# Attention in steps of two items: scores and outputs of a pair share PSUM banks, and the order of a step is rewritten

## The chip, the cores and the metric

One core of a Trainium2 chip. The metric is the device time of one execution in microseconds (us). Engines: PE is TensorE (matmuls; transposes are matmuls with an identity), DVE is VectorE, ACT is ScalarE, POOL is GpSimd, SP issues DMAs. Every engine works through its own queue in order and waits there for semaphores of the others.

## What is computed

Attention in a window of 128 positions over q, k, v of shape (4, 8, 576, 64), then a mixture of 8 experts whose gate is balanced over all tokens, then a dense block:

```
scores = where(0 <= i - j < 128, q k^T / 8 - slope_h |i - j|, -1e9)
x      = softmax(scores) v                        # 2304 tokens x 512
P      = exp(x w_gate - max); 8 times: P /= rows, P /= columns, P *= N / E
x      = sum_e P[:, e] * (relu(x w1[e]) w2[e])
out    = g(x w_in) w_out                          # g: 0, (h + 1)^2 / 4, h
```

## The kernel before

To keep float32 accuracy every large matmul is three: an operand is kept as a high part (fp32r) and a low part, and high x high, low x high and high x low add up in one PSUM bank (`mm3`, lines 72 to 75).

**Attention** goes by items (g, i): g is one of 16 pairs of heads (4 batches x 4 pairs), i one of 5 blocks of query rows (4 of 128 rows, the last of 64); 80 items. One item passes through five stages, each a function:
- `a_scores` (S): for each of two heads three matmuls over 64 rows of the array, into one bank per head (`s0`, `s1`); then on DVE per head one instruction that adds the bias and takes the row maximum (line 290), and a small negation (293).
- `a_exp` (E): two exps on ACT (300). `a_norm` (N): 1/sum on DVE (306, 307), multiplication on POOL (308).
- `a_turn` (T): transposes of the weights on PE (320), copied out by ACT (first key block, 324) and DVE (second, 326).
- `a_out` (O): weights times v on PE, each head into 64 columns of the array (338); high part of the result on ACT (341), low part on DVE (342).

Beside them run `a_prep` (P: transposes of q and k on PE, line 264, one bank `p`; high parts on ACT, 270; low parts on DVE, 271), in three parts per pair of heads; B, which advances the splitting of weights for the first expert (ACT line 78, POOL line 79); and F, the **fill-in**: groups of three matmuls of the first expert's first half (`u0_g1`, `u0_g2`) and of the gate (`logits`: lines 351 and 358), which need only tokens whose attention is done. `blocks` says after which item each block of tokens may start, `credit` and `SHARE` how many groups a step gets. What fill-in is left runs after attention; then come the other experts and the dense block, bound by PE.

The order is written by hand: step s works on item s in S, on s - OE in E, s - ON in N, s - DT in T and s - DO in O, in the order of the letters of `START` (first 19 steps) or `ORDER`; `PREP0` and `PREP` say at which step each preparation stands.

Of the kernel before, what the change touches and what calls it, by code (L numbers as in the profile page):

```python
# [19 lines left out]
P = 128  # L20
# [8 lines left out]
def attn_moe_ffn(ctx: ExitStack, tc, q, k, v, w_gate, w1, w2, w_in, w_out, out):  # L29
# [243 lines left out]
    def a_scores(g, i, ap, bias):  # L273
        h0 = 2 * (g % NPAIR)
        q0, nq = QB[i]
        k0 = max(0, q0 - P)
        nk = q0 + nq - k0
        c0 = P if i == 0 else 0
        s = ap.tile([P, 2, 2 * P], F32, tag="s", bufs=DT + 1, name="s")
        mx = ap.tile([P, 8], F32, tag="mx", bufs=DT + 2, name="mx")  # L280
        (qh, ql), (kh, kl) = QK[g, "q"], QK[g, "k"]
        pss = []
        for j in range(2):
            hs = slice(j * D, (j + 1) * D)
            ps = ps_pools[0].tile([P, 2 * P], F32, tag=f"s{j}", bufs=1, name="pss")
            pss.append(ps)
            mm3(ps[:nq, :nk], qh[hs, q0:q0 + nq], ql[hs, q0:q0 + nq], kh[hs, k0:k0 + nk], kl[hs, k0:k0 + nk],
                True, True)
        for j in range(2):
            nc.vector.tensor_tensor_reduce(  # L290
                out=s[:nq, j, :nk], in0=pss[j][:nq, :nk], in1=bias[:nq, h0 + j, c0:c0 + nk], scale=1.0,
                scalar=-3.0e38, op0=ALU.add, op1=ALU.max, accum_out=mx[:nq, j:j + 1])
        nc.vector.tensor_scalar(mx[:nq, 2:4], mx[:nq, 0:2], -1.0, None, ALU.mult)
        st[g, i] = (s, mx, nk)
# [16 lines left out]
    def a_turn(g, i, ap):  # L311
# [4 lines left out]
        at = ap.tile([P, 2, 2, P], F32, tag="at", bufs=DO - DT + 1, name="at")  # L316
# [12 lines left out]
    def a_out(g, i):  # L329
        b, hp = divmod(g, NPAIR)  # L330
        q0, nq = QB[i]
        at, kbs = atT.pop((g, i))
        o = ps_pools[0].tile([P, P], F32, tag="o", bufs=1, name="pso")
        for j in range(2):
            hs = slice(j * D, (j + 1) * D)
            for c, kb in enumerate(kbs):
                n = QB[kb][1]
                nc.tensor.matmul(o[hs, :nq], lhsT=nat[b, "v", kb][:n, (2 * hp + j) * D:(2 * hp + j + 1) * D], rhs=at[:n, c, j, :nq],  # L338
                                 start=(c == 0), stop=(c == len(kbs) - 1))
        cs = slice(b * SQ + q0, b * SQ + q0 + nq)  # L340
        nc.scalar.activation(xh[:, hp, cs], o[:, :nq], AF.Copy)
        nc.vector.tensor_tensor(xl[:, hp, cs], o[:, :nq], xh[:, hp, cs].bitcast(F32), ALU.subtract)
# [396 lines left out]
    DT, DO, OE, ON = 3, 4, 1, 1  # L739
    START, ORDER, NSTART = "EBSNFPOT", "BFESNPFOT", 19  # L740
    SHARE = 1.8
    PREP0 = [-1, 3, 4, 0, 5, 6, 1, 7, 8, 2, 9, 10]
    PREP = [11, 14, 17, 20, 29, 34, 37, 41, 53, 56, 59, 67]
    LAG = (5, 4, 4, 4, 4, 4, 6, 4)
    with tc.manual_schedule():
# [11 lines left out]
        preps = [(y, *divmod(n, 3)) for n, y in enumerate(PREP0)]  # L757
        preps += [(PREP[g - NPAIR] + x, g, x) for g in range(NPAIR, NG) for x in range(3)]
# [9 lines left out]
        with tc.tile_pool(name="ac", bufs=1, side="right") as ac, tc.tile_pool(name="ap", bufs=2, side="right") as ap, \  # L768
# [8 lines left out]
            ri = ap.tile([P, 2 * P], mybir.dt.int32, tag="s", bufs=DT + 1, name="ri")  # L777
# [34 lines left out]
            gated = []  # L812
# [12 lines left out]
            work, credit, step = unit0(), 0.0, [0]  # L825
            for s in range(NI + DO):
                step[0] = s
                order = START if s < NSTART else ORDER
                for op_ in order:
                    off = {"S": 0, "E": OE, "N": ON, "T": DT, "O": DO}.get(op_, 0)  # L830
                    if not 0 <= s - off < NI and op_ in "SENTO":
                        continue
                    g, i = items[min(s - off, NI - 1)]
                    if op_ == "S":
                        a_scores(g, i, ap, bias)
                        if s < 2:
                            for h in range(2, 6) if s == 0 else range(6, H):
                                make_bias(h)
                        if s == 3:
                            for x in range(NPAIR, NPAIR + 2):  # L840
                                a_load(x, ap)
                        if s == 2:
                            fast.append(u0_weights(wp))
                        if s == 9:
                            fast.append(gate_setup())
                    elif op_ == "E":
                        a_exp(g, i)
                    elif op_ == "N":
                        a_norm(g, i)
                    elif op_ == "T":  # L850
                        a_turn(g, i, ap)
# [9 lines left out]
                    elif op_ == "P":  # L861
                        if s == max(PREP0) + 1:
# [3 lines left out]
                        for _, pg, x in (y for y in preps if y[0] == s):  # L866
# [3 lines left out]
                    elif op_ == "O":  # L870
                        a_out(g, i)
                        if (g + 1) % NPAIR == 0 and g + 1 < NG:
                            for x in [i - 1] if i < NQ - 1 else [i - 1, i]:
                                if x >= 0:
                                    v_load((g + 1) // NPAIR, x, ap)
            while state == "open":
                state = next(work)
            step[0] = 2 * NI
# [96 lines left out]
```

## Time and profile before

| | us |
|---|---|
| median of 3 runs | 2126.49 (2126.47 to 2130.02) |
| the profiled execution, its own time | 2127.65 |
| its span in the profile | 2125.9 |
| PE, DVE, ACT, POOL busy | 2085.9, 1318.9, 672.1, 615.5 |

The page gives means over the whole span. The attention part is its first 255 us; there the busy time of an engine is to be read by stretches, and a matmul by the distance from its start to the next one's: matmuls are pipelined, so the length of one (0.28 us for 256 columns) is longer than what it costs in a run.

### The profile page before, as it was taken

Reading aid. Unit: us, or ns where it says so; the run is one execution under the profiler, and the core shown is the slowest. Engines: PE = TensorE matmul, PEld = TensorE weight load, DVE = VectorE, ACT = ScalarE, POOL = GpSimd, SP = SyncE. Lnnn points to the kernel's source line nnn. Section 1 sums busy time; section 2 is a strip of 40 time slices with the busy share of each in tenths; the row PEclk is TensorE's granted clock in tenths of the full one; section 3 lists DMA queues with packets and bytes.
Section 4 is the critical chain, followed back from the end, with each engine's and each line's share of the span. In section 5 each row is a group of like instructions: output and inputs, shape, how many; then the busy total and the mean of one; then the engine's idle time right before and its main releaser. Section 6 shows DMA issues by size and latency. Waiting matters only on the chain.

```text
span 2125.9 us, 30586 instructions
## 1 busy us (share of the span) xinstructions
PE 2085.9 (98%) x11187; PEld 1838.8 (86%) x11187; DVE 1318.9 (62%) x2999; ACT 672.1 (32%) x1601; POOL 615.5 (29%) x619
## 2 busy tenths in 40 slices
PE   8999999999999999999999999999999999999999
PEld 5777779998998898998998899899899988888887
DVE  6766484544454666666665765766665567767665
ACT  6666534333333332121121132121121133232322
POOL 4332226666666631011111110111110022232322
PEclk9999999999999999999999999999999999999999
DMA  7322136767677676766676566676665445464542
GB/s 140 76 70 60 42 124 255 280 249 257 240 266 265 209 265 245 256 244 223 240 249 223 214 226 241 242 257 232 225 242 208 175 177 183 169 221 154 204 183 104
DMA packets 179622, 432.46 MB, mean 203 GB/s; under 512 B 69648, under 2 KB 93200, under 8 KB 179472
## 3 DMA queue, kind: packets, MB, share of 16 engines
q1 hardware_dynamic: 168112, 411.37, 55.2%
q10 hardware_dynamic: 11360, 19.14, 2.8%
q8 instruction: 88, 1.44, 0.3%
q14 instruction: 62, 0.51, 0.1%
HBM read 311.44 MB, written 119.01 MB: 202 GB/s over the span
## 4 chain that ended last, share of the span: by engine, by line
PE 88%; DVE 7%; ACT 2%; DMA 1%; issue 1%; POOL 0%; DVEq 0%; ACTq 0%; POOLq 0%
PE psg L73 16%; PE psg L75 15%; PE psg L74 15%; PE psc L73 3%; PE psd L73 3%; PE psc L74 3%; PE psd L74 3%; PE psc L75 3%; PE psd L75 3%; PE pso L338 3%; PE psa L74 3%; PE psa L75 3%; PE psa L73 3%; PE psb L73 2%; PE psb L74 2%; PE psb L75 2%
## 5 line engine op out<-in xcount | busy, mean ns | idle before, releaser
L75 PE MATMUL psg<-w2h,hl 128*128 128x512 f32 x1368 | 534.5, 391 | 0.8 <-POOL hl L628 0.5
L73 PE MATMUL psg<-w2h,hh 128*128 128x512 f32 x1368 | 533.7, 390 | 0.9 <-DVE acc L686 0.9
L74 PE MATMUL psg<-w2l,hh 128*128 128x512 f32 x1368 | 532.3, 389 | 0.0
L686 DVE SCALAR_TENSOR_TENSOR acc<-psg,pt,acc 128x512 f32<-128x512 f32 x252 | 188.1, 749 | 254.4 <-PE psg L75 252.8
L75 PEld LDWEIGHTS psg<-w2h,hl 128*128 128x128 f32 x1368 | 256.8, 188 | 58.6 <-POOL hl L628 5.4
L73 PEld LDWEIGHTS psg<-w2h,hh 128*128 128x128 f32 x1368 | 256.8, 188 | 51.5 <-DVE acc L686 1.3
L74 PEld LDWEIGHTS psg<-w2l,hh 128*128 128x128 f32 x1368 | 256.9, 188 | 51.0
L628 POOL TENSOR_TENSOR hl<-g,hh 128x384 fp32r<-128x384 f32 x96 | 111.6, 1171 | 280.7 <-ACT hh L626 262.0
L73 PE MATMUL psc<-xh,w1h 128*128 128x384 f32 x456 | 156.5, 343 | 17.9 <-DVE u L641 17.9
L615 ACT ACTIVATE hh<-c 128x384 fp32r<-128x384 f32 x270 | 140.8, 522 | 88.6 <-DVE c L652 57.7
L617 DVE SCALAR_TENSOR_TENSOR hl<-c,hh 128x384 fp32r<-128x384 f32 x270 | 160.1, 626 | 0.0
L75 PE MATMUL psc<-xh,w1l 128*128 128x384 f32 x456 | 154.8, 340 | 0.0
L74 PE MATMUL psc<-xl,w1h 128*128 128x384 f32 x456 | 154.7, 339 | 0.0
L73 PE MATMUL psd<-sh,w1h 128*128 128x384 f32 x456 | 153.5, 337 | 0.8 <-DVE c L644 0.8
L74 PE MATMUL psd<-sl,w1h 128*128 128x384 f32 x456 | 153.0, 336 | 0.0
L75 PE MATMUL psd<-sh,w1l 128*128 128x384 f32 x456 | 152.9, 335 | 0.0
L79 POOL TENSOR_TENSOR dl<-e,dh 128x128 fp32r<-128x128 f32 (+1 forms) x64 | 43.1, 682 | 356.7 <-ACT dh L78 356.7
L635 ACT ACTIVATE p<-psa 128x384 f32<-128x384 f32 x57 | 28.1, 493 | 343.1 <-PE psa L75 340.9
L308 POOL TENSOR_TENSOR s<-s,mx 128x512 f32<-128x512 f32 (+2 forms) x80 | 72.9, 911 | 153.1 <-DVE mx L307 70.0
L79 POOL TENSOR_TENSOR w2l<-raw,w2h 128x512 fp32r<-128x512 f32 x60 | 81.3, 1377 | 104.4 <-ACT w2h L78 104.4
L73 PEld LDWEIGHTS psc<-xh,w1h 128*128 128x128 f32 x456 | 85.6, 188 | 22.3 <-DVE u L641 22.2
L638 DVE TENSOR_TENSOR u<-psb,p 128x384 f32<-128x384 f32 x57 | 31.8, 557 | 116.5 <-PE psb L75 96.5
(198 smaller groups left out, 4183.1 us busy)
## 6 DMA issues: line engine op xcount, KB each, us to landing
w1h<-wd1h SPq DMA_DIRECT2D x84, 896.0 KB, 4.6
w1l<-wd1l SPq DMA_DIRECT2D x84, 896.0 KB, 6.8
w2h<-wd2h SPq DMA_DIRECT2D x84, 512.0 KB, 5.1
w2l<-wd2l SPq DMA_DIRECT2D x84, 512.0 KB, 6.2
raw<-in_moe_w SPq DMA_DIRECT2D x60, 512.0 KB, 4.5
wd1h<-w1h SPq DMA_DIRECT2D x30, 896.0 KB, 6.2
wd1l<-w1l SPq DMA_DIRECT2D x30, 896.0 KB, 6.4
wd2h<-w2h SPq DMA_DIRECT2D x30, 512.0 KB, 6.2
```

What stands on the lines that cost most here:

```text
L73: nc.tensor.matmul(ps, lhsT=lh, rhs=rh, start=first, stop=False, skip_group_check=on)
L74: nc.tensor.matmul(ps, lhsT=lh, rhs=rl, start=False, stop=False, skip_group_check=on)
L75: nc.tensor.matmul(ps, lhsT=ll, rhs=rh, start=False, stop=last, skip_group_check=on)
L79: eng.tensor_tensor(l, x, h.bitcast(F32), ALU.subtract)
L308: nc.gpsimd.tensor_tensor(s[:nq, :, :nk], s[:nq, :, :nk], mx[:nq, 6:8].unsqueeze(2).to_broadcast([nq, 2, nk]), ALU.mult)
L338: nc.tensor.matmul(o[hs, :nq], lhsT=nat[b, "v", kb][:n, (2 * hp + j) * D:(2 * hp + j + 1) * D], rhs=at[:n, c, j, :nq], start=(c == 0), sto ...
L615: nc.scalar.activation(h, c, AF.Relu)
L617: V.scalar_tensor_tensor(l, c, 0.0, h.bitcast(F32), ALU.max, ALU.subtract)
L628: nc.gpsimd.tensor_tensor(l, g, h.bitcast(F32), ALU.subtract)
L635: nc.scalar.activation(p1, pa, AF.Copy)
L638: V.tensor_tensor(u2, pb, p1, ALU.add)
L686: nc.vector.scalar_tensor_tensor(a, ps, sc, a, ALU.mult, ALU.add)
```

## The change

A step now takes two items that follow one another. `a_scores` writes both items' scores of a head into one bank, head by head in turn, then reduces the two items; `a_out` writes both items' outputs into one bank, then takes high and low part of the first item and of the second. E, N and T run their two items one after the other. A step's order is S, T, P, N, E, B, P, O at first and S, T, P, N, E, F, B, F, P, O from step 6 on; exps belong to the same step as the scores (OE 0), turn and outputs to the one two steps back. At the first P one preparation part runs, at the last P all others that are due. Fill-in gets 3.6 groups a step and starts after the last preparation of the first batch is done (step 10).

```diff
+    def a_scores(two, ap, bias):
+        PS = [ps_pools[0].tile([P, 2, 2 * P], F32, tag=f"s{j}", bufs=1, name="pss") for j in range(2)]
...
+        for x, (g, i) in enumerate(two):
...
+            for n, (a, b) in enumerate(((qh, kh), (qh, kl), (ql, kh))):
+                for j in range(2):
+                    hs = slice(j * D, (j + 1) * D)
+                    nc.tensor.matmul(PS[j][:nq, x, :nk], lhsT=a[hs, q0:q0 + nq], rhs=b[hs, k0:k0 + nk],
+                                     start=n == 0, stop=n == 2)
+        for x, (g, i) in enumerate(two):
...
+            s = ap.tile([P, 2, 2 * P], F32, tag="s", bufs=6, name="s")
+            mx = ap.tile([P, 8], F32, tag="mx", bufs=8, name="mx")
...
-        at = ap.tile([P, 2, 2, P], F32, tag="at", bufs=DO - DT + 1, name="at")
+        at = ap.tile([P, 2, 2, P], F32, tag="at", bufs=4, name="at")
...
+    def a_out(two):
+        PS = ps_pools[0].tile([P, 2, P], F32, tag="o", bufs=1, name="pso")
+        for x, (g, i) in enumerate(two):
...
+                    nc.tensor.matmul(PS[hs, x, :nq], lhsT=nat[b, "v", kb][:n, (2 * hp + j) * D:(2 * hp + j + 1) * D],
+                                     rhs=at[:n, c, j, :nq], start=(c == 0), stop=(c == len(kbs) - 1))
+        for x, (g, i) in enumerate(two):
...
+            nc.scalar.activation(xh[:, hp, cs], o, AF.Copy)
+            nc.vector.tensor_tensor(xl[:, hp, cs], o, xh[:, hp, cs].bitcast(F32), ALU.subtract)
...
-    DT, DO, OE, ON = 3, 4, 1, 1
-    START, ORDER, NSTART = "EBSNFPOT", "BFESNPFOT", 19
-    SHARE = 1.8
-    PREP0 = [-1, 3, 4, 0, 5, 6, 1, 7, 8, 2, 9, 10]
+    DT, DO, OE, ON = 2, 2, 0, 1
+    START, ORDER, NSTART = "STPNEBPO", "STPNEFBFPO", 6
+    SHARE = 3.6
+    PREP0 = [-1, 2, 3, 0, 3, 4, 1, 5, 6, 2, 7, 8]
     PREP = [11, 14, 17, 20, 29, 34, 37, 41, 53, 56, 59, 67]
...
-        preps += [(PREP[g - NPAIR] + x, g, x) for g in range(NPAIR, NG) for x in range(3)]
+        preps += [((PREP[g - NPAIR] + x) // 2, g, x) for g in range(NPAIR, NG) for x in range(3)]
...
-                    while step[0] <= last + DO:
+                    while step[0] <= max(last // 2 + DO, max(PREP0) + 1):
...
-                        for _, pg, x in (y for y in preps if y[0] == s):
+                        now = [y for y in preps if y[0] <= s]
+                        for y in now[:1 if pos < order.rindex("P") else None]:
+                            preps.remove(y)
+                            _, pg, x = y
                             a_prep(pg, ap, x)
```

Smaller edits: the last six bias rows are all made in step 0, the loads of the second batch's first pairs and the weight splits are put in at step 1, the gate's setup at step 4.

Where the instructions stand, at three places. First PE in the middle of attention, between fill-in of 512 columns (psg; pss are scores, psat turned weights, pso outputs). Before, one item:

```order
L75 MATMUL psg<-w1h,hl 128x512
L73 MATMUL pss<-xl 128x256
...
L75 MATMUL pss<-xl 128x256
L73 MATMUL psg<-w1h,hh 128x512
...
L75 MATMUL psg<-w1h,hl 128x512
L338 MATMUL pso<-at,nv_138 64x64
...
L320 MATMUL psat<-ident,s 128x128 x2
L73 MATMUL psg<-w1h,hh 128x512
```

and now the end of one step and the start of the next:

```order
L75 MATMUL psg<-w1h,hl 128x512
L343 MATMUL pso<-at,nv_1064 64x128 [waits DVE_49,Activation_49]
L343 MATMUL pso<-at,nv_1161 64x128 [waits DMAHW2_49,DVE_49]
...
L343 MATMUL pso<-at,nv_1161 64x128 [waits Activation_49]
...
L286 MATMUL pss<-xh 128x256 x12
L324 MATMUL psat<-ident,s 128x64 [waits PE_49,Pool_49]
...
L324 MATMUL psat<-ident,s 128x128 [waits PE_49,Pool_49]
...
L264 MATMUL pst<-ident,nq 128x128 [waits DMAHW4_49]
...
L73 MATMUL psg<-w1h,hh 128x512
```

Scores of two items now follow outputs directly and lead straight into the turn; no fill-in stands between them.

Second, ACT's queue in one of the first steps. Before (item step; L300 are the exps, L270 the preparation, L341 the outputs' high part):

```order
L324 ACTIVATE at<-psat 128x256 [waits PE_49,Activation_49]
L300 ACTIVATE s,mx<-s,mx 128x256 [waits DVE_49,Pool_49]
...
L78 ACTIVATE w1h<-raw 128x512
L354 ACTIVATE L<-psl 16x256 [waits PE_49]
L270 ACTIVATE xh<-pst 128x512 [waits PE_49]
L341 ACTIVATE xh<-pso 128x128 [waits PE_49]
```

and now, step 5 (the same names, the exps on L304, the outputs on L350):

```order
L328 ACTIVATE at<-psat 128x256 [waits PE_49,Activation_49] x2
L270 ACTIVATE xh<-pst 128x256 [waits PE_49]
L270 ACTIVATE xh<-pst 128x256 [waits DVE_49]
L304 ACTIVATE s,mx<-s,mx 64x192 [waits Pool_49]
...
L304 ACTIVATE s,mx<-s,mx 128x256 [waits Pool_49]
...
L78 ACTIVATE w0h<-raw 128x512 [waits DMAHW0_49]
L270 ACTIVATE xh<-pst 128x512 [waits PE_49]
L350 ACTIVATE xh<-pso 128x128 [waits PE_49]
L350 ACTIVATE xh<-pso 128x128 [waits DVE_49]
```

The exps stood ahead of a step's preparation and now stand behind its first part, whose second copy waits for DVE; the second item's output copy waits for DVE too.

Third, DVE's queue of the same step (L294 reductions, L330 copy of turned weights, L271 preparation, L351 outputs' low part):

```order
L330 COPY at<-psat 128x256 [waits Activation_49]
L271 SCALAR_TENSOR_TENSOR xh<-pst,xh 128x256 [waits Activation_49] x2
L310 TENSOR_SCALAR mx<-mx 128x2
L311 RECIPROCAL mx<-mx 128x2 [waits DVE_49]
...
L271 SCALAR_TENSOR_TENSOR xh<-pst,xh 128x512 [waits Activation_49]
L351 TENSOR_TENSOR xl<-pso,xh 128x128 [waits Activation_49] x2
L294 ISA s,mx<-pss,bias 128x256 [waits PE_49,Pool_49]
```

The next step's first reduction (the last row) stands behind both low parts of this step's outputs.

## Rows read from the trace of the kernel before

**Rows 1.** The page, busy time of each engine with its share and instructions.

```profile
PE 2085.9 (98%) x11187; PEld 1838.8 (86%) x11187; DVE 1318.9 (62%) x2999; ACT 672.1 (32%) x1601; POOL 615.5 (29%) x619
```

**Rows 2.** Stretches: PE, PEld, DVE, ACT, POOL busy, PE clock, DMA.

```profile
7.30:41.40 34.10, 29.93 (x162) 20.91 (x162) 24.88 (x108) 20.98 (x77) 13.86 (x14) 1.00 0.84 166
...
68.90:243.60 174.70, 174.70 (x1429) 127.83 (x1428) 117.57 (x577) 114.85 (x419) 53.59 (x60) 1.00 0.24 60
...
276.90:280.40 3.50, 3.10 (x7) 2.48 (x8) 3.26 (x10) 1.94 (x4) 2.36 (x3) 0.51 0.38 147
```

**Rows 3.** Timeline of PE: first score matmuls of items 0, 20, 79; a spacing early.

```profile
7.30 0.47 PE L73 MATMUL pss<-xh 64*128 64x128 f32 x1 [1.35 <-ACT xh L270]
...
30.04 0.42 PE L74 MATMUL pss<-xl 64*128 64x256 f32 x2
30.26 0.42 PE L75 MATMUL pss<-xl 64*128 64x256 f32 x2
...
68.93 0.33 PE L73 MATMUL pss<-xh 64*128 64x128 f32 x2
...
243.61 0.31 PE L73 MATMUL pss<-kh,qh 64*64 64x192 f32 x2
```

**Rows 4.** Timeline of PE: start, length, instruction (xN: merged); lone groups, then a run.

```profile
152.55 0.39 PE L73 MATMUL pss<-xh 64*128 64x256 f32 x2
152.78 0.29 PE L74 MATMUL pss<-xh 64*128 64x256 f32 x2
152.89 0.28 PE L75 MATMUL pss<-xh 64*128 64x256 f32 x2
153.11 0.39 PE L73 MATMUL psg<-xh,w0h 128*128 128x256 f32 x1
...
153.67 0.67 PE L338 MATMUL pso<-at,nv 128*64 128x128 f32 x8
...
270.10 0.28 PE L73 MATMUL psg<-xh,w0h 128*128 128x256 f32 x1
...
270.44 0.28 PE L73 MATMUL psg<-xh,w0h 128*128 128x256 f32 x1
```

**Rows 5.** Timeline of DVE, then of ACT: one item's reductions and exps.

```profile
150.89 0.42 DVE L290 CUSTOM_DVE_ANT_0 s<-pss,bias 128x256 f32<-128x256 f32 x1 [0.76 <-PE pss L75]
...
151.78 0.16 DVE L306 TENSOR_SCALAR mx<-mx 128x2 f32<-128x2 f32 x1
...
150.22 0.50 ACT L300 ACTIVATE s<-s,mx 128x256 f32<-128x256 f32 x1
...
151.35 0.38 ACT L433 ACTIVATE hh<-psg 128x256 fp32r<-128x256 f32 x1
```

**Rows 6.** Groups by line and shape, 100 to 250 us: count, busy us, mean ns.

```profile
L342 DVE TENSOR_TENSOR xl<-pso,xh 128x128 fp32r<-128x128 f32 x41 | 11.7, 286 | 6.4 <-ACT xh L341 5.8
L341 ACT ACTIVATE xh<-pso 128x128 fp32r<-128x128 f32 x41 | 11.3, 277 | 14.5 <-PE pso L338 14.1
L271 DVE SCALAR_TENSOR_TENSOR ql<-pst,qh 128x512 fp32r<-128x512 f32 x6 | 4.1, 680 | 0.1
L270 ACT ACTIVATE qh<-pst 128x512 fp32r<-128x512 f32 x6 | 3.6, 594 | 1.0 <-PE pst L264 1.0
```

**Rows 7.** Timeline of ACT and DVE: a preparation of two matrices in one bank.

```profile
24.01 0.62 ACT L78 ACTIVATE w0h<-raw 128x512 fp32r<-128x512 f32 x1
24.95 0.38 ACT L270 ACTIVATE xl<-pst 128x256 fp32r<-128x256 f32 x1 [0.32 <-PE pst L264]
26.62 0.38 ACT L270 ACTIVATE xl<-pst 128x256 fp32r<-128x256 f32 x1 [1.29 <-DVE xl L271]
...
27.04 0.42 DVE L271 SCALAR_TENSOR_TENSOR xl<-pst,xl 128x256 fp32r<-128x256 f32 x1 [0.45 <-ACT xl L270]
```

**Rows 8.** Timeline of PE, 275 to 278 us: the waits before the clock fell.

```profile
275.30 0.50 PE L75 MATMUL psg<-w1h,hl 128*128 128x512 f32 x1 [1.58 <-DVE hl L434]
...
277.30 0.79 PE L75 MATMUL psg<-w1h,hl 128*128 128x512 f32 x1 [1.04 <-DVE hl L434]
```

More of the change, by code (lines that the diff above doesn't have):

```diff
@@ L271, in a_prep @@
             nc.vector.scalar_tensor_tensor(l, pc, scale, h.bitcast(F32), ALU.mult, ALU.subtract)
[L273 to L294, printed above, removed]
+    def a_scores(two, ap, bias):
+        PS = [ps_pools[0].tile([P, 2, 2 * P], F32, tag=f"s{j}", bufs=1, name="pss") for j in range(2)]
+        made = []
+        for x, (g, i) in enumerate(two):
+            q0, nq = QB[i]
+            k0 = max(0, q0 - P)
+            nk = q0 + nq - k0
+            made.append((nq, nk, P if i == 0 else 0))
+            (qh, ql), (kh, kl) = QK[g, "q"], QK[g, "k"]
+            for n, (a, b) in enumerate(((qh, kh), (qh, kl), (ql, kh))):
[4 more added lines that the diff above has]
+        for x, (g, i) in enumerate(two):
+            nq, nk, c0 = made[x]
+            h0 = 2 * (g % NPAIR)
+            s = ap.tile([P, 2, 2 * P], F32, tag="s", bufs=6, name="s")
+            mx = ap.tile([P, 8], F32, tag="mx", bufs=8, name="mx")
+            for j in range(2):
+                nc.vector.tensor_tensor_reduce(
+                    out=s[:nq, j, :nk], in0=PS[j][:nq, x, :nk], in1=bias[:nq, h0 + j, c0:c0 + nk], scale=1.0,
+                    scalar=-3.0e38, op0=ALU.add, op1=ALU.max, accum_out=mx[:nq, j:j + 1])
+            nc.vector.tensor_scalar(mx[:nq, 2:4], mx[:nq, 0:2], -1.0, None, ALU.mult)
+            st[g, i] = (s, mx, nk)
@@ L756, in attn_moe_ffn @@
         NI = len(items)
-        preps = [(y, *divmod(n, 3)) for n, y in enumerate(PREP0)]
-        preps += [(PREP[g - NPAIR] + x, g, x) for g in range(NPAIR, NG) for x in range(3)]
+        preps = [(y, *divmod(n, 3)) for n, y in enumerate(PREP0) if n]
+        preps += [((PREP[g - NPAIR] + x) // 2, g, x) for g in range(NPAIR, NG) for x in range(3)]
         blocks = [(7, 0, 256), (19, 256, 256), (27, 512, 256), (39, 768, 384), (47, 1152, 256), (59, 1408, 256),
@@ L775, in attn_moe_ffn @@
                 v_load(0, i, ap)
[L777 removed]
+            ri = ap.tile([P, 2 * P], mybir.dt.int32, tag="s", bufs=6, name="ri")
             nc.gpsimd.iota(ri, pattern=[[1, 2 * P]], base=-P, channel_multiplier=-1)
@@ L861, in attn_moe_ffn @@
                     elif op_ == "P":
-                        if s == max(PREP0) + 1:
+                        if s == max(PREP0) + 1 and not opened:
+                            opened.append(s)
                             p0.close()
@@ L870, in attn_moe_ffn @@
                     elif op_ == "O":
[L871 to L875, printed above, removed]
+                        a_out(two)
+                        for g, i in two:
+                            if (g + 1) % NPAIR == 0 and g + 1 < NG:
+                                for x in [i - 1] if i < NQ - 1 else [i - 1, i]:
+                                    if x >= 0:
+                                        v_load((g + 1) // NPAIR, x, ap)
             while state == "open":
                 state = next(work)
-            step[0] = 2 * NI
+            step[0] = NI
         spool = ctx.enter_context(tc.tile_pool(name="spool", bufs=1, side="right"))
```

56 lines of the change are left out of this document (28 added, 28 removed).

## The prediction, made before the changed kernel had run

> **What bounds the kernel now.** I read the page's busy times first. TensorE is busy 98% of the span and VectorE and ScalarE have much room [rows 1]; but these are means over stages, so I went to the stretches of the attention part next [rows 2], cut at the first score matmul of item 0, where that spacing halves, and at the first score matmuls of items 20 and 79 [rows 3]. The reader is to see three stages. From 7.3 to 41.4 us PE is busy 88% of the time although it has no fill-in yet, and at the lower of its two rates: score matmuls of 256 columns start 0.22 us apart at 30 us, 0.11 us apart at 152 us [rows 3, 4]. From 68.9 to 243.6 us, 59 items of attention with fill-in, PE shows no gap (174.7 of 174.7 us), while DVE and ACT are busy two thirds of it: this stage is bound by PE's issue, at 174.7 / 59 = 2.96 us an item. After it comes the dense mixture of experts, which the change does not touch.
>
> Then the single matmuls of one item, start to start [rows 4]. Three fill-in matmuls of 256 columns in a run take 0.34 us (270.10 to 270.44). The same three between scores and outputs take 0.56 us (153.11 to 153.67), and so does the score triple, whose two heads run side by side on 64 rows each (152.55 to 153.11). So what PE loses is at the borders between kinds of matmul: full array, two row halves (scores), two column halves (outputs). A lone group loses 0.22 us by its two borders, some 0.1 us on either side of each, and a border has two sides.
>
> **What the change saves on PE.** An item has four borders now: fill-in to scores, scores to fill-in, fill-in to outputs, outputs to turn (turn to fill-in is none: both use the full array). At 0.2 us for a border with scores or fill-in on both sides, and 0.15 for those of outputs and turn, whose first matmul is held up less, that is 0.7 us an item. After the change a step of two items has three: outputs to scores 0.2, scores to turn 0.15, fill-in to outputs 0.15, together 0.5, or 0.25 an item. It saves 0.45 an item, 0.9 a step: PE's own need falls from 2 x 2.96 = 5.92 us to 5.0 us a step. Matmuls, reductions, copies and bytes stay the same in number. The interleaving of the two heads' score matmuls costs and gains nothing, since the two heads already start 0.01 us apart (the x2 of these rows).
>
> **What it adds: two waits in series that PE's work now has to cover.** The exps come in the same step as the scores (OE 0 for 1), behind the step's first preparation in ACT's queue; the next step's reductions come behind the low parts of this step's outputs in DVE's queue; and two items share a bank. Durations, from X, the start of a step's first reduction on DVE:
> - Reductions and negation of one item hold DVE 0.89 us (150.89 to 151.78), of two 1.78; each reads a bank that is ready only after both items' scores. The exps of one item hold ACT about 1.0 us, 1.13 with the tail (150.22 to 151.35) [rows 5]; of two 2.1.
> - Outputs: high part on ACT 0.28, low part on DVE 0.28 [rows 6], and now high of the second item only after low of the first: 4 x 0.28 and hand-overs, 1.2 us.
> That last wait has a forerunner in the trace: of a preparation with two matrices in one bank, ACT's second copy stood 1.29 us until DVE had read the first, and DVE then waited 0.45 us for ACT [rows 7]. The page PSUM — Partial Sum Buffer of the Trainium skill (section on PSUM bank collisions) says that two engines must not touch the same bank and partitions at once, reads included, so that software orders them; the order of these rows agrees. If the two items' outputs could be read side by side, 1.2 would be 0.9, and the sum below would be 12 us lower over 40 steps.
>
> **Steps 0 to 9, without fill-in.** First fill-in moves from item step 12 to double step 10. A step's chain: reductions 1.78; the second item's copy, 0.36; low part of q, 0.41; then ACT's copy of k, 0.38 [rows 7], which waits for it; so the exps, which could start at X + 1.0, start at X + 3.0 and end at 5.1; a weight split on ACT, 0.62 [rows 7], 5.7; outputs 1.2, 6.9 us to the next X. Pairs with the short item 0 take less; I take 6.6. Preparations that stand at the second place, after the exps, come on top: a first one 1.3 (ACT 0.6 and DVE 0.68 [rows 6], in front of the outputs' parts), a second 2.4, since it has one bank and goes transposes, ACT, DVE one after the other. Seven of the ten steps have one, three of them two. Sum: the first reductions at 9.3 (first scores at 7.3 [rows 3], two items of them at the low rate), 10 x 6.6, 7 x 1.3, 3 x 2.4, less 3 splits (1.9) and two steps without outputs (2.4), plus six bias rows on DVE in step 0 (2.1): X of step 10 at 89.4, its scores 1.4 earlier, at 88.0. Before, item 20 was scored at 68.9 [rows 3]. **Loss 19 us**. Bounds: 14 if a third of the late preparations hides, 26 if PE at its low rate ends each step's scores some 0.7 us after the low parts.
>
> **Steps 10 to 39.** The chain without preparation: copies done at X + 2.5, the second item's outputs on PE and their end 3.5, parts 1.2: 4.8, about PE's need; I take 4.9. With one wide preparation first, ACT's 0.6 comes ahead of the exps (start X + 1.5, end 3.6), then the fill-in's copy and DVE's 0.68: 5.4. With one narrow one (two matrices of 64 columns) the wait for DVE is as in steps 0 to 9: 6.7. With two, the late one adds its hand-overs: 5.9 to 7.5, mean 6.2. By the table PREP, 14 steps have none, 4 one wide, 1 one narrow, 11 two: 14 x 4.9 + 4 x 5.4 + 6.7 + 11 x 6.2 = 165 us, against 60 x 2.96 = 178: **gain 13 us** of the 27 that PE alone would give. Bounds: 5.2 us a step (gain 22) and 5.8 (gain 4), PE's need plus a little and today's pace less a little.
>
> **Small terms.** The gate's second matmul now follows its first at once in four of five blocks; it needs an ACT copy behind the exps (ready at X + 3.4, PE there at some X + 1.3), and what is late anyway in such a step hides half: +4 us (0 to 9). By order 105 fill-in groups stand before the last outputs against 110, five of 0.35 us are left for later: +2. The two closing steps come even, as do DMA queues: the loads of the next pairs and values are the same and issued at the same items. POOL's two normalisations in a row end before the next negation; nothing.
>
> **Sum:** 19 - 13 + 4 + 2 = +12 us. The profiled execution took 2127.65 us, with a span of 2125.9; it would be about 2140. The median of the runs is 1.2 lower, 2126.49, so I predict 2138.7 us.
>
> **Rivals.**
> A. *PE stays the bound.* For it: PE has no gap in 175 us now, with DVE and ACT at two thirds [rows 2]. Against it: the exps now stand behind preparation in ACT's queue. It decides where a step's chain is under 5.0 us with preparations too, that is, if ACT gets to the exps by X + 1. Then no loss in steps 0 to 9, gain 30 x 0.9 = 27, +2: about 2101 us, faster.
> B. *The two sides cancel.* A loss of 14 early, a gain of 20 later, +4, +2: within 4 us of before, 2126.
> C. *The clock falls.* PE went to the lower of its two levels (1.2 of 2.4 GHz; granted 0.51 from 276.9 to 280.4 us [rows 2]) after it had waited 1.58 us and then 1.04 us close together [rows 8]. Such a stretch of 3.5 us loses 1.75 us. In the eleven steps with two preparations PE waits 1 to 2.5 us; if each brings one such stretch, that is 19 us, and with a rise some 12 us later than now, at half rate, 6 more: 25 us above my sum, about 2164. Against it: PE there runs ahead of the chain, so half of the lower rate falls into the wait. The Trainium skill's page TensorE: Matmul & The Clock Gate (Loop structure and HAM oscillation) speaks against this change in the same way, that pauses between bursts of matmuls put the clock back; rows 8 agree for one place.
>
> **Chances.** My sum 0.60; A 0.14; B 0.15; C 0.11. A change under 0.2% (4.3 us) is about what this kernel's measurement cannot tell from none. So faster 0.14, same 0.15, slower 0.71. The range runs from 14 - 22 + 0 + 2 = -6, 2120, to 26 - 4 + 9 + 2 = +33, 2160, and holds B; it leaves out A and the larger half of C, about 2 in 10.
>
> **What would show it.** Right: ACT's exps in the first steps released by DVE after preparation; item 20's scores near 88 us; PE gaps of about 0.5 us a step from 90 us on, before outputs and before late transposes, put down to DVE; the gate's second matmul waiting for ACT some 2 us; last outputs near 259 us. The lone score triples gone from PE's list, 0.9 us less PE time a step. Wrong: PE without gaps from 90 us on and step 10 before 75 us (A); a granted clock of 0.5 in several stretches after step 12 (C).

## The result, and the profile after

The change makes the kernel slower: 2154.63 us (median of 5 runs, 2151.54 to 2157.82) against 2126.83 for the kernel before on the same chip (5 runs, 2126.47 to 2130.02), a ratio of 1.0128 with a 95% interval of 1.0113 to 1.0144: 28 us, 24 to 31 by the interval. Forecast were 12. Direction and range held, the size did not.

The profiled execution took 2157.82 us (span 2156.1), 30.2 more than the one before; it is the slowest of the five and has the lowest mean granted clock of them (0.983, the others 0.986 to 0.988). First the page of the kernel after (busy times; of the forty slices, PE's busy tenths and granted clock), to be read beside [rows 1]:

```profile
PE 2079.8 (96%) x11187; PEld 1853.9 (86%) x11187; DVE 1310.9 (61%) x2999; ACT 672.6 (31%) x1601; POOL 614.0 (28%) x619
...
PE   6799989999999999999999999999999999999999
...
PEclk8599999999999999999999999999999999999999
```

PE is busy 6 us less in all and the span 30 us longer. Busy and clock are low together in the first two slices, some 108 us. So I cut both kernels at the same six places: first score matmul of items 0, 10, 20, 24 and 78 (after: steps 0, 5, 10, 12 and 39), last output matmul, first matmul of the next expert (tile psa). Windows view (stretch, length, busy us of PE, PEld, DVE, ACT, POOL with instructions, granted clock, DMA share, GB/s), the kernel before:

```profile
7.30:40.20 32.90, 28.73 (x151) 19.86 (x151) 23.72 (x103) 19.88 (x73) 13.14 (x14) 1.00 0.87 170
40.20:68.90 28.70, 28.39 (x260) 22.05 (x259) 23.71 (x111) 22.20 (x82) 13.85 (x14) 1.00 0.26 59
68.90:81.90 13.00, 13.00 (x102) 9.43 (x101) 8.77 (x43) 7.75 (x30) 3.46 (x5) 1.00 0.45 103
81.90:240.80 158.90, 158.90 (x1308) 116.26 (x1307) 107.23 (x526) 105.87 (x384) 48.92 (x54) 1.00 0.23 58
240.80:254.50 13.70, 13.49 (x104) 9.87 (x104) 6.22 (x28) 6.46 (x24) 3.45 (x4) 1.00 0.00 0
254.50:314.10 59.60, 53.91 (x300) 44.58 (x301) 42.22 (x107) 18.48 (x36) 18.07 (x15) 0.97 0.37 133
```

and after:

```profile
7.70:39.20 31.50, 22.41 (x140) 16.67 (x140) 18.63 (x91) 15.36 (x58) 6.10 (x7) 0.84 0.81 143
39.20:90.10 50.90, 32.68 (x217) 25.53 (x216) 25.65 (x116) 26.62 (x94) 17.48 (x18) 0.61 0.20 53
90.10:109.30 19.20, 17.76 (x111) 14.65 (x109) 8.78 (x43) 8.45 (x31) 5.73 (x6) 0.61 0.27 60
109.30:259.90 150.60, 143.33 (x1299) 117.62 (x1297) 101.51 (x525) 104.69 (x382) 47.91 (x54) 0.99 0.25 59
259.90:274.00 14.10, 13.64 (x118) 10.90 (x117) 6.35 (x31) 6.70 (x23) 3.85 (x4) 1.00 0.35 113
274.00:344.90 70.90, 61.37 (x345) 52.11 (x346) 43.68 (x115) 19.46 (x40) 17.81 (x15) 0.95 0.26 97
```

The differences, which add up to the 30.2 (from first psa to the end both kernels take 1811.2 to 1811.8 us of span):

| stretch | before | after | difference | forecast |
|---|---|---|---|---|
| to the first scores of item 20 | 68.9 | 90.1 | +21.2 | +19 |
| steps 10, 11 | 13.0 | 19.2 | +6.2 | in the next row |
| steps 12 to 38 | 158.9 | 150.6 | -8.3 | -13 + 4, for steps 10 to 39 |
| step 39 to the last outputs | 13.7 | 14.1 | +0.4 | 0 |
| last outputs to first psa | 59.6 | 70.9 | +11.3 | +2 |

The loss up to item 20 lies in steps 5 to 9: 50.9 us for 28.7. PE did 217 matmuls there for 260; before, 39 of the 260 were fill-in and 12 the gate's, for which these steps have no place now. The waits of PE in that stretch (releaser, us in total, times, longest; "issue" means that the profile shows no releaser), after:

```profile
PE pst L264 <- DVE xl L271: 5.8, 3, 2.5
PE pst L264 <- issue: 5.8, 2, 3.4
PE pst L264 <- DVE xh L271: 5.8, 3, 2.7
PE psat L324 <- POOL s L312: 0.9, 2, 0.6
```

Before, from 40.2 to 68.9, the one wait listed is of 0.3 us. All but 0.9 of the waits now stand in front of transposes of a preparation. The two put down to issue end where the others do, 0.10 and 0.11 us after the previous preparation's last low part on DVE; the loads that they could have waited for had landed before (at 30.1 and 61.1 us). The second of them, with that low part:

```profile
63.67 0.42 DVE L271 SCALAR_TENSOR_TENSOR xl<-pst,xl 128x256 fp32r<-128x256 f32 x1 [0.45 <-ACT xl L270]
64.20 1.09 PE L264 MATMUL pst<-ident,nq 128*128 128x128 f32 x4 [2.44 <-issue]
```

One of the other waits in the timeline of the kernel after (start, length, instruction, in brackets the idle time before it and who ended it), step 6:

```profile
51.14 0.22 PE L264 MATMUL pst<-ident,fk 64*128 64x64 f32 x1
...
51.41 0.22 ACT L270 ACTIVATE xh<-pst 128x64 fp32r<-128x64 f32 x1
...
51.60 0.74 DVE L330 COPY at<-psat 128x256 f32<-128x256 f32 x2
52.27 0.21 DVE L271 SCALAR_TENSOR_TENSOR xh<-pst,xh 128x64 fp32r<-128x64 f32 x1
52.51 0.22 ACT L270 ACTIVATE xh<-pst 128x64 fp32r<-128x64 f32 x1 [0.88 <-DVE xh L271]
52.63 0.50 ACT L304 ACTIVATE s<-s,mx 128x256 f32<-128x256 f32 x1
52.77 0.23 DVE L271 SCALAR_TENSOR_TENSOR xh<-pst,xh 128x64 fp32r<-128x64 f32 x1 [0.29 <-ACT xh L270]
...
53.05 0.66 PE L264 MATMUL pst<-ident,nk 128*128 128x128 f32 x4 [1.69 <-DVE xh L271]
...
55.01 0.57 ACT L270 ACTIVATE xh<-pst 128x512 fp32r<-128x512 f32 x1
...
56.36 0.36 PE L264 MATMUL pst<-ident,nq 64*128 64x64 f32 x1 [2.66 <-DVE xh L271]
```

The transposes of a preparation are ready to be read at 51.4. Their first low part stands behind two copies of turned weights on DVE (51.60 to 52.27), ACT's second high part behind that low part (0.88 us), the exps behind that high part, and PE, which wants to write the next preparation's transposes into bank p, behind the second low part (1.69). Then the next preparation's high part stands behind the exps and a weight split on ACT (55.01), and PE waits 2.66 us more. In this step three preparations pass through one bank one after the other, each with ACT, DVE and PE in turn. This is the chain of the forecast. PE's clock was granted at 0.61 on average over the stretch and at half from 64.0 to 94.7 us without a break; it fell again from 98.1 to 108.3 us, with PE busy throughout:

```profile
64.00:94.70 30.70, 23.29 (x138) 18.54 (x139) 13.80 (x65) 14.39 (x51) 9.34 (x9) 0.50 0.22 57
98.10:108.30 10.20, 10.20 (x61) 8.18 (x60) 4.60 (x22) 4.11 (x16) 2.45 (x3) 0.50 0.25 56
```

So PE at half rate is what steps 10 and 11 met. The tail holds more fill-in than before: the third matmuls of its groups by width (count, busy us, mean ns, idle time before them), before and after; the sixteen groups of 384 columns are the same in both.

```profile
L75 PE MATMUL psg<-w1h,hl 128*128 128x512 f32 x33 | 14.2, 429 | 3.1 <-DVE hl L434 3.1
L75 PE MATMUL psg<-xh,w0l 128*128 128x256 f32 x32 | 8.9, 277 | 0.0
...
L75 PE MATMUL psg<-w1h,hl 128*128 128x512 f32 x36 | 15.9, 442 | 7.2 <-DVE hl L443 7.1
L75 PE MATMUL psg<-xh,w0l 128*128 128x256 f32 x43 | 12.0, 279 | 0.0
```

The pauses and the low clock had to be told apart, and the tail's 11 us to be explained.

### The profile page after: what moved, and what is told of

It is laid out like the page before. It is cut to its first block, busy times and chain, and to the rows that moved or that the text cites. A ratio compares the mean times of both kernels' runs of the same rounds, so it can differ in the third digit from the quotient of the medians.

```text
span 2156.1 us, 30525 instructions
## 1 busy us (share of the span) xinstructions
PE 2079.8 (96%) x11187; PEld 1853.9 (86%) x11187; DVE 1310.9 (61%) x2999; ACT 672.6 (31%) x1601; POOL 614.0 (28%) x619
## 4 chain that ended last, share of the span: by engine, by line
PE 86%; DVE 8%; ACT 3%; issue 1%; DMA 1%; POOL 1%; ACTq 0%; DVEq 0%; POOLq 0%
PE psg L75 15%; PE psg L73 15%; PE psg L74 15%; PE psc L73 3%; PE psc L74 3%; PE psc L75 3%; PE psd L73 3%; PE psd L74 3%; PE psd L75 3%; PE psa L74 3%; PE psa L75 3%; PE psa L73 3%; PE psb L73 2%; PE psb L74 2%; PE psb L75 2%; PE pso L343 2%
## 5 line engine op out<-in xcount | busy, mean ns | idle before, releaser
L75 PE MATMUL psg<-w2h,hl 128*128 128x512 f32 x1368 | 534.4, 391 | 0.8 <-POOL hl L637 0.5
L75 PEld LDWEIGHTS psg<-w2h,hl 128*128 128x128 f32 x1368 | 256.7, 188 | 58.5 <-POOL hl L637 5.4
L75 PE MATMUL psc<-xh,w1l 128*128 128x384 f32 x456 | 154.8, 340 | 0.0
L75 PE MATMUL psd<-sh,w1l 128*128 128x384 f32 x456 | 152.9, 335 | 0.0
```

The lines of the kernel that those rows point to most:

```text
L75: nc.tensor.matmul(ps, lhsT=ll, rhs=rh, start=False, stop=last, skip_group_check=on)
```

## Experiments

Theory: the one bank of the early preparations, and the order of ACT and DVE in it, makes the loss of steps 5 to 9; fill-in that finds no place is paid after attention; the low clock follows from the pauses. Rivals: the low clock itself makes the loss (rival C); or PE's own work does. In what follows "item 20" is the time of its first scores (90.1 after), "steps 12 to 38" and "tail" (last outputs to first psa) are stretches of the profiled execution. Kernels of each run are compared with the kernel before at 2127.5 to 2128.2 us. The intervals of the changed kernel's variants reach 3 to 4 us to either side, so totals of theirs that differ by less than some 5 us are not told apart.

**1. Order of the preparation alone.** Both matrices' high parts first, then both low parts:

```diff
             nc.scalar.activation(h, pc, AF.Copy, scale=scale)
+        for nm, i0, i1, c0 in todo:
...
             nc.vector.scalar_tensor_tensor(l, pc, scale, h.bitcast(F32), ALU.mult, ALU.subtract)
```

> In a_prep both high parts on ACT come first and both low parts on DVE after them, so ACT's exps no longer wait for DVE through a preparation with two matrices in one bank. Series theory (exps held by DVE through that bank): the exps of steps 0 to 9 start some 1.5 us earlier a step, item 20 is scored at about 78 us instead of 90.1, a few us more are won at narrow preparations later: about 2139 us, 15 us under the changed kernel. Rival, low clock: steps 0 to 9 are long because PE runs at its lower rate there; item 20 stays at 88 to 90 us and the time within 3 us of the changed kernel. Rival, late preparations: what makes these steps long are the parts after the exps in one bank; 2 to 4 us are won.

Measured 2145.18 us (2139.19 to 2148.89), ratio 1.0079 (1.0061 to 1.0097); item 20 at 85.4, not the 78 expected. The turns between ACT and DVE inside a preparation are worth 5 us up to item 20, a quarter of its loss; the forecast had priced them higher.

**2. The same for the outputs**, both items' high parts, then both low parts:

```diff
             nc.scalar.activation(xh[:, hp, cs], o, AF.Copy)
+        for x, (g, i) in enumerate(two):
...
             nc.vector.tensor_tensor(xl[:, hp, cs], o, xh[:, hp, cs].bitcast(F32), ALU.subtract)
```

> In a_out both items' high parts come first, then both low parts: one hand-over between ACT and DVE instead of three in the shared bank. Series theory: 0.35 us less in each of the 40 steps that end in this chain: 3 us less up to item 20, and between 3 us (where PE ends most steps) and 10 us less in steps 10 to 39; about 2147 us. Rival, PE bound from step 12 on: under 4 us in all, nearly all before item 20.

Measured 2151.23 us (2150.02 to 2152.72), ratio 1.011 (1.0093 to 1.0127); item 20 at 86.8, steps 12 to 38 at 5.57 us each for 5.58. So 3 us early and nothing later: the forecast's remark that outputs read side by side would save 12 us over 40 steps finds no support in this order with fewer turns.

**3. Clock held up by idle work.** Three matmuls of the identity with a bias row, whose result nobody reads, in each of steps 2 to 9:

```diff
                         advance(fast, 2)
+                        if 2 <= s <= max(PREP0) + 1:
+                            for _ in range(3):
+                                wm = ps1.tile([P, 512], F32, tag="g", bufs=2, name="warm")
+                                nc.tensor.matmul(wm[:, :2 * P], lhsT=ident, rhs=bias[:, 0, :], start=True, stop=True)
```

> Three more matmuls of ident with a bias row (128 x 256, float32, result not used) in each of steps 2 to 9, where PE waits some 2.7 us a step. Clock theory: PE is at its upper rate in most of steps 2 to 11; steps 10 and 11 take 12 us instead of 19.2, and up to 5 us more are won before: about 2145 us, last outputs near 264 us. Series theory: steps 0 to 9 are not shortened by a faster PE (item 20 at 88 to 92 us), only steps 10 and 11 gain; if the clock were of no account at all, the time would be the same or up to 5 us longer.

Measured 2149.26 us (2146.42 to 2151.72), ratio 1.01 (1.0085 to 1.0115). Steps 5 to 9 in the windows view:

```profile
37.80:86.00 48.20, 35.10 (x247) 27.66 (x246) 25.50 (x115) 26.10 (x94) 17.22 (x17) 0.82 0.21 53
```

The granted clock rose from 0.61 to 0.82, though not to full, and the steps lost 2.7 of their 50.9 us. Run 5 below took 36.7 us for the same steps at a lower clock, 0.72. Rival C, as the main cause of the early loss, falls.

**4. More fill-in a step.**

```diff
-    SHARE = 3.6
+    SHARE = 4.2
```

> SHARE 4.2 instead of 3.6: 19 more fill-in groups run inside attention and 19 fewer after it. If PE has slack within the steps from 10 on (its gaps of 7 us in 150, and waits the profile does not show), the stretch after the last outputs shrinks by about 8 us and attention grows by less: 2 to 5 us won, about 2151 us. If PE is the bound from step 12 on, the time stays within 2 us of the changed kernel, and the 14 groups that were left over cost what they take, about 6 us, wherever they stand.

Measured 2149.24 us (2145.29 to 2153.95), ratio 1.0101 (1.0081 to 1.0122). Steps 5 to 9, steps 10 and 11, steps 12 to 38, and tail:

```profile
38.70:89.60 50.90, 32.86 (x219) 25.62 (x218) 25.66 (x116) 26.60 (x94) 17.50 (x18) 0.61 0.21 52
89.60:103.60 14.00, 12.22 (x114) 10.33 (x112) 7.95 (x42) 7.75 (x29) 4.72 (x6) 0.95 0.29 64
103.60:258.10 154.50, 149.86 (x1353) 123.90 (x1351) 102.28 (x528) 107.08 (x387) 47.79 (x54) 1.00 0.26 62
...
274.00:332.60 58.60, 49.73 (x285) 42.64 (x285) 41.15 (x104) 17.45 (x35) 18.75 (x15) 0.97 0.36 131
```

Two readings. Steps 5 to 9 are the same to the tenth, at the same low clock; yet steps 10 and 11 took 14.0 us for 19.2, with a granted clock of 0.95 for 0.61. So the clock costs some 5 us there; whether the edit kept it up, or only this execution, is not shown. And with 19 groups of fill-in fewer left over (11 of 256 and 8 of 512 columns), the tail fell by 12.3 us, of which steps 12 to 38 took back 3.9 and the steps after them 1.8.

**5. Three banks for early preparations.** Preparations take banks p, g, g in turn; the two g banks serve the fill-in, which starts at step 10.

```diff
-        ps = ps_pools[0].tile([P, 512], F32, tag="p", bufs=1, name="pst")
+        if S.get("early", -1) >= 0:
+            S["early"] += 1
+        if S.get("early", -1) % 3 > 0:
+            ps = ps_pools[0].tile([P, 512], F32, tag="g", bufs=2, name="pst")
+        else:
+            ps = ps_pools[0].tile([P, 512], F32, tag="p", bufs=1, name="pst")
...
+                if s == 0:
+                    S["early"] = 0
+                elif s == max(PREP0) + 2:
+                    S.pop("early")
```

> Preparations of steps 0 to 9 take turns among three banks (their own and the two that fill-in will use from step 10 on); nothing else changes. If the late preparations in one bank make the first steps long (PE waited 1.69 us and 2.66 us for DVE in step 6), these waits go: steps 6 to 8 take 9, 10.5 and 9.5 us instead of 10.4, 12.4 and 11.0, item 20 is scored at 84 to 86 us instead of 90.1, about 2149 us. If the chain through ACT and DVE is as long without PE's wait, since the work of three parts stands between exps and outputs anyway, under 2 us are won.

Measured 2152.61 us (2150.41 to 2155.31), ratio 1.0118 (1.0103 to 1.0133). Item 20 came at 75.4, ten us earlier than expected. The total says that the bank is nothing; the stretches say otherwise. Steps 5 to 9, then 12 to 38:

```profile
38.70:75.40 36.70, 30.29 (x217) 22.60 (x216) 23.93 (x112) 23.55 (x89) 15.55 (x15) 0.72 0.29 72
...
92.60:258.50 165.90, 150.34 (x1300) 121.38 (x1299) 102.35 (x525) 105.87 (x382) 47.91 (x54) 0.96 0.22 53
```

and PE's waits in the second:

```profile
PE psg L73 <- DVE kl L276: 5.1, 5, 1.7
PE pst L269 <- DVE hl L448: 2.6, 5, 0.9
PE psg L73 <- DVE ql L276: 2.2, 3, 1.1
```

Steps 5 to 9 gained 14.2 us, steps 12 to 38 lost 15.3. The edit did more than I meant: after `pop` the default of -1 gives 2 modulo 3, so every preparation from step 10 on stood in the g banks, and fill-in waited for the low parts of q and k and transposes for the fill-in's (hl). Run 13 mends it.

**6. Exps a step later and ahead of scores**, so that they need no fresh reduction:

```diff
-    DT, DO, OE, ON = 2, 2, 0, 1
-    START, ORDER, NSTART = "STPNEBPO", "STPNEFBFPO", 6
+    DT, DO, OE, ON = 2, 2, 1, 1
+    START, ORDER, NSTART = "ESTPNBPO", "ESTPNFBFPO", 6
```

> OE 1 and the exps at the head of a step, as before the change (orders E S T P N B P O and E S T P N F B F P O); the paired scores and outputs stay. Series theory: exps and reductions of one step then run beside each other on ACT and DVE; a step without late parts falls from about 7 to 5.5 us, item 20 is scored at 75 to 80 us, the rest as in the changed kernel: about 2142 us. Rival, low clock or late preparations: item 20 stays at 86 us or more, about 2151 us.

Measured 2150.47 us (2148.2 to 2155.04), ratio 1.0112 (1.0095 to 1.0129); item 20 at 85.0, where 75 to 80 was expected and 86 or more by the rival; steps 5 to 9 at 46.4 us.

**7. All four** (1, 2, 5, 6) with fill-in at 4.2.

> Exps first, three banks for early preparations, high parts first in preparations and outputs, SHARE 4.2. If the losses are the ones named, and each is removed once, they add up: item 20 at 72 to 76 us, step 12 at 85, PE's saving of 0.3 us a step (5.58 against 5.88) then stands alone, and the time is 2118 to 2130 us, near the kernel before. If PE's lower rate up to 100 us is what holds it, about 2138 us.

Measured **2120.31 us** (2119.4 to 2122.91), ratio 0.9968 (0.9956 to 0.998): 34 us below the change, 7 below the kernel before. Item 20 at 58.2, the start of step 12 at 72.4, where 72 to 76 and 85 were expected: the total fell into its range only because steps 12 to 38 were 10.5 us longer than after the change. From the first clock record, at 23.8 us, full clock was granted up to 269 us. **8** is the kernel before with edit 1 alone:

> The kernel before, with only the high parts first in preparations. There the exps stand ahead of the preparations and PE has no gap after 41 us, so the wait through the shared bank is covered: same time within 2 us (2127.8), item 20 at 68 to 69 us. If it were a cost of its own, not one that the new order uncovers, it would save about as much as in the changed kernel, 9 us.

Measured 2123.93 us (2122.08 to 2126.34), ratio 0.9981 (0.9972 to 0.9991): 4 us for a line moved, neither the same time nor the 9 us of the changed kernel. Items 0 to 9 took 26.9 us for 32.9 and items 10 to 19 33.0 for 28.7, while the first clock record, at full clock, stands at 23.7 us for 41.4 and the clock fell to half from 37.4 to 44.2; how much of the 4 us is the order and how much the clock is not shown.

**9 to 11. One part taken back from the four-part kernel**: the fill-in (3.6), the banks, the exps' place.

> The four-part kernel (exps ahead of scores, three banks for the early preparations, both high parts first in preparation and output, 4.2 groups of fill-in a step) with the fill-in back at 3.6 groups a step. Theory (left-over fill-in is paid one for one after the last outputs, whatever the early steps do): last outputs some 4 us earlier than in the four-part kernel, first psa 8 to 10 us after that difference, 2124 to 2128 us in all. Rival (what 4.2 gained was only that a denser PE kept the clock up in the early steps): stretches of half clock return before 110 us, over 2135 us.

> The four-part kernel with all early preparations back in the one bank p. Theory (the early steps are bound by the chain of preparations through one bank: transposes, ACT, DVE, next transposes; the low clock follows from the pauses): first scores of step 10 at 72 to 82 instead of 58.2, half clock again in the early steps, 2135 to 2142 us. Rival (the exponentials' place and the high-first orders had already shortened the chain; the bank alone buys nothing, as its run alone said, 2 us): first scores of step 10 within 4 us of 58.2, 2120 to 2125 us.

> The four-part kernel with the exponentials back in their own step (scores first in the step). Theory (banks first, the exponentials' wait for the reductions is a smaller one of the pauses): first scores of step 10 at 62 to 68, clock full or with one low stretch, 2122 to 2130 us. Rival (the pause between a step's scores and its exponentials is the one that lets the clock fall): half clock over 20 us or more of the early steps, first scores of step 10 past 72, 2135 us or more.

| kernel | median (range), us | steps 5 to 9 | item 20 | steps 12 to 38 | tail |
|---|---|---|---|---|---|
| four parts | 2120.31 (2119.4 to 2122.91) | 26.1 | 58.2 | 161.1 | 58.5 |
| 9, fill-in back | 2127.92 (2124.38 to 2131.38) | 26.1 | 58.4 | 156.7 | 69.3 |
| 10, banks back | 2129.86 (2128.74 to 2132.01) | 42.1 | 76.8 | 152.2 | 59.7 |
| 11, exps back | 2130.32 (2128.48 to 2134.22) | 27.9 | 61.7 | 163.2 | 60.4 |

Run 9 leaves the early steps alone, so the left-over fill-in is a term by itself (11 us in the tail, 4 in the steps). Run 10 gives the bank: 16.0 us in steps 5 to 9, after 14.2 when it was the only edit. Its total was forecast at 2135 or more and came out lower, because taking the banks back also took back what they cost in steps 12 to 38 (161.1 to 152.2): the same fault. Run 11 lost 10 us, of them only 1.8 in steps 5 to 9; steps 10 and 11 took 20.3 us for 14.3, with the clock at half from 68.1 to 81.8 us. In steps 5 to 9 the four edits 5, 6, 1 and 2, each alone, save 14.2, 4.5, 2.8 and 2.6 us, 24.1 together, and all four at once 24.8: there they about add up.

**12. The kernel before with what it can take of this** (edits 1 and 5, and 2.1 groups an item).

> The kernel before (steps of one item) with the parts that it can take: three banks for the early preparations, both high parts first in the preparation, and 2.1 groups of fill-in an item (4.2 for two). Theory (steps of two items save 0.3 us in 5.9 a step and no more, and the rest of the four-part kernel's 7.5 us come from these parts): 2119 to 2123 us, level with or a little above the four-part kernel's 2120.3. Rival (steps of two items are what gains, once the early steps run): stays at the 2123.9 of the order of the preparation alone, or above.

Measured 2127.74 us (2127.06 to 2132.32), ratio 1.0005 (0.9995 to 1.0014): a miss for the theory, and spoilt by the fault of 5, since its items of steps 12 to 38 took 171.2 us for 158.9.

**13 to 16. The banks for the early preparations alone**, later ones in p, in four kernels: the change with only this edit; the four-part kernel; the same with 4.8 groups; the kernel before, with edit 1 and its own fill-in.

```diff
-        if S.get("early", -1) % 3 > 0:
+        if S.get("early", 0) % 3 > 0:
```

> The change with the preparations of steps 0 to 9 over three banks (p, g, g) and all later ones in p, as they were. The run with banks p, g, g did more than its edit said: from step 10 on every preparation stood in the two g banks, which the fill-in shares, and its steps 12 to 39 took 165.9 us against 150.6. Theory (the one bank of the early preparations is the largest part of the loss in steps 5 to 9; the 15 us were given back because fill-in and preparations met in g): first scores of step 10 near 75, steps 12 to 39 again 150 to 152 us, 2136 to 2141 us in all. Rival (steps 12 to 39 were longer for the clock, or because work that the early steps no longer hid came later): steps 12 to 39 stay over 160 us, 2148 us or more.

> The four-part kernel with the preparations from step 10 on back in p. Theory: the PE waits for ql and kl ahead of fill-in in steps 12 to 39 (some 6 us) go, 2111 to 2116 us. Rival (PE is the bound there and the waits only change their name, to transposes that wait for the one bank p): within 2 us of 2120.3.

> The same with 4.8 groups of fill-in a step. Theory (fill-in is worth moving into the steps only as far as PE pauses there; with 4.2 few pauses are left): within 3 us of the kernel with 4.2. Rival (each group left over costs its whole time after the last outputs, and little inside the steps): another 4 to 8 us faster.

> The kernel before with the preparations of its early steps over three banks, later ones in p, both high parts first, and its own 1.8 groups an item. Theory (before, PE waits little in the early steps, so banks and order are worth little more than the order alone): 2119 to 2124 us, so that with these cares steps of two items are 5 us or more ahead. Rival (the gain of the four-part kernel is that of the banks, whichever way the steps are cut): 2116 us or less.

| kernel | median (range), us | ratio to before (interval) | item 20 | steps 12 to 38 | tail |
|---|---|---|---|---|---|
| 13, change with banks | 2142.6 (2136.95 to 2144.51) | 1.0062 (1.0043 to 1.0081) | 74.9 | 151.5 | 73.1 |
| 14, four parts | **2110.58** (2110.15 to 2111.36) | 0.9919 (0.9904 to 0.9934) | 58.3 | 152.1 | 59.8 |
| 15, with 4.8 | 2115.55 (2113.96 to 2116.74) | 0.9941 (0.9927 to 0.9956) | 58.5 | 161.4 | 48.1 |
| 16, before | 2121.62 (2119.26 to 2123.63) | 0.997 (0.9958 to 0.9982) | 64.4 | 158.8 | 59.6 |

The bank alone is worth 12 us of the 28 that the change lost; run 13's stretches fell into the ranges expected, its total 1.6 us above. The four-part kernel with it beats the change by 44 us and the kernel before by 17. Its stretches (steps 0 to 4, 5 to 9, 10 and 11, 12 to 38, tail):

```profile
6.50:32.20 25.70, 20.03 (x140) 14.96 (x140) 19.10 (x95) 14.40 (x58) 6.07 (x7) 1.00 1.01 185
32.20:58.30 26.10, 21.74 (x218) 16.57 (x218) 25.23 (x109) 21.98 (x85) 15.53 (x15) 1.00 0.42 102
58.30:71.50 13.20, 11.97 (x115) 9.78 (x114) 10.08 (x47) 8.11 (x31) 7.25 (x8) 1.00 0.30 67
71.50:223.60 152.10, 149.40 (x1352) 123.72 (x1351) 103.29 (x528) 98.20 (x386) 47.93 (x55) 1.00 0.26 63
...
238.90:298.70 59.80, 51.34 (x285) 43.88 (x286) 40.32 (x104) 17.38 (x35) 18.54 (x15) 0.94 0.35 128
```

PE pauses 2.7 us in steps 12 to 38 here, 7.3 after the change. Run 15 missed both expectations: the tail fell by 11.7 us, steps 12 to 38 rose by 9.3, and 6 us were lost behind the first psa, where PE then waited 4.6 us for DVE's u (tile psc), a wait that run 14 has not. Fill-in is cheap inside a step as long as PE pauses there: the step from 3.6 to 4.2 groups cost 3.9 us in steps 12 to 38 (run 4), the one to 4.8 cost 9.3, for 14 and 15 groups and one block of the gate each; four of the 14 and eight of the 15 had 512 columns, the others 256, so the second lot was also heavier. Run 14 is 11 us ahead of run 16. That is not the price of steps of two items alone, because run 14 also has edit 2 and 4.2 groups a step, which run 9 priced at 7.6 us; the kernel before with 2.1 groups an item and only the early banks was not run.

## Why the forecast was right, and where it was not

- **The early loss** (+19, measured +21.2): right, and by its mechanism, if not in its parts. Preparations with one bank were the step's late part; the exps were released after a preparation's DVE part; item 20 was scored at 90.1 for 88.0. By the terms of the sum step 5 was due at 41 to 43 us and came at 39.2; steps 5 to 9 were due to take 45 to 47 us and took 50.9, so errors partly cancelled. Runs 5, 10 and 13 show that the bank is the larger part of it (14 to 16 us in steps 5 to 9), runs 1, 2 and 6 that the turns between ACT and DVE and the exps' place are about the rest; the 16 us that the forecast gave to the late preparations fit the bank's share, and the hold of the exps, 2 us a step in the forecast, was worth less. The page PSUM — Partial Sum Buffer of the Trainium skill (section on PSUM bank collisions) has ACT and DVE ordered on one bank, reads too; the 0.88 us for which ACT's second high part waited for DVE's first low part, whose result it does not use, agrees, and so does the gain from other banks.
- **Steps 10 to 39** (-13 + 4 = -9): steps 12 to 38 gave -8.3. PE's work fell by 15.6 us in these 27 steps (158.9 to 143.3 us busy, with 1308 and 1299 matmuls), 0.58 a step where I had 0.9, so a border seems to be worth less than the 0.2 and 0.15 us that I took; 7.3 us of pauses gave half of it back, 0.27 a step where my chain had 0.5. Two errors of like size against each other: that the sum fits is luck. The gate's second matmuls waited 4.7 us for ACT over the whole kernel, as forecast (+4).
- **Fill-in left over** (+2, measured +11.3): the step that failed. Twice: its count and its price. By order I had 110 groups before the last outputs in the kernel before and 105 in the changed one, five left. The traces have 357 and 315 matmuls of fill-in there, 119 and 105 groups, fourteen left: my count of the kernel before was nine short. Before, thirteen groups stood in items 10 to 19, where the change allows none. And a group left over cost 0.8 us, not 0.35, which is the price of 256 columns in a run: three of the fourteen have 512 columns (0.70 us), and there were 7.5 us more PE work in the tail, of it some at half clock, and 3.8 us more of pauses (waits for hl, the low part that DVE makes of the expert's hidden values, at psg L75: 7.1 us, before 3.1). Run 9 against 7 moved such groups into the steps and out again, and the tail followed by 11 us.
- **The clock** (0 in my sum, 25 in rival C with a chance of 0.11): the second step that failed, a term put at nothing, in steps 10 and 11, 6.2 us. Run 4, with the same steps 0 to 9, had a higher clock there and needed 5.2 us less; run 6, at full clock there, took 12.3 us. Whole executions show it too: run 4's four took 2145.3 and 2145.5 us at a mean granted clock of 0.989, 2152.9 and 2154.0 us at 0.983. As the main cause of the early loss rival C is refuted (run 3); that pauses put the clock back fits the runs. After the change PE waited up to 3.4 us at a time in steps 5 to 9 and the clock swung between its two levels (0.61 on average); in run 14, with no wait above 0.8 us there, it stayed at 1.00. The Trainium skill's page TensorE: Matmul & The Clock Gate has a section on PSUM-queue cycling, by which short pauses between groups of matmuls are enough for the clock to swing. The granted 0.61 agrees; in run 14 PE paused too, 4.4 of 26.1 us in steps 5 to 9, and the clock did not swing.
- **Rival A** (PE stays the bound, 2101) was wrong for the change. The kernel with four parts and early banks came nearer to it, 2110.58, with PE pausing 2.7 us in steps 12 to 38; it also has more fill-in a step.

In sum: early +21.2 for +19, steady -8.3 for -9, clock +6.2 for 0, tail +11.3 for +2, the rest -0.2. The sign that last outputs would come near 259 us did not follow from the sum, which gives 254.5 + 19 - 9 = 264.5; they came at 274.0. What stays open is why a border costs PE less than the forecast's rows said, and why the clock fell again at 98 us after the change and not in the profiled execution of run 4.

## What to carry to other kernels

A step with no place for fill-in loses twice: its own pauses, and the groups that it used to hide, which cost more in the drain than in the steps; count them in the traces, not by a reading of the order. Before several things that are made in turn pass ACT and DVE through one bank, give them the banks that later work doesn't yet use, and give these back when it does. Judge an edit by its stretches: of the bank's 14 us the total showed 2, because the same edit lost 15 elsewhere.

## What the runs showed of the hardware beyond this

- When TensorE's clock first rose doesn't follow from how busy PE was. Before, score matmuls of 256 columns started 0.22 us apart at 30 us and 0.11 at 152 [rows 3, 4], although PE was busy 28.7 of 32.9 us in items 0 to 9. In run 14, with 20.0 of 25.7 us busy, the twelve of the step at 27.4 us started within 0.70 us, as at full rate later (0.68; at half rate 1.24, so at 58.7 us after the change). But run 12, busy 22.7 of 24.7 us, was at full rate by 22 us; and run 4, whose first ten steps are those of the change, had its first clock record at 36.3 us where the change had it at 23.0.
- The granted clock column says 1.00 up to 41.4 us of the kernel before [rows 2], where the matmuls' spacing shows the lower rate. The trace has no clock record before that time, and the column counts a time without record as 1.00. At the start it is the spacing that has to be read.
